# Two attention layers with Fourier mixing: the first transposes, the order of loads and values in the prologue, and the last sums

## The chip, the cores and the metric

The kernel runs on one core of one Trainium2 chip. Its time is device microseconds of one execution; the figure for a kernel is the median of several runs. The core has five engines that each take their own instructions in order: TensorE (PE, its weight loads shown as PEld), VectorE (DVE), ScalarE (ACT), GpSimd (POOL) and SyncE (SP, which here only issues DMA). Engines wait for each other through semaphores. Before the change the median of three runs is 2556.03 us (2554.49 to 2556.99).

## What is computed

Two layers, and each layer is an attention block followed by a Fourier mixing block, both on normalized rows and both added to the residual. There are 2048 rows of 640 columns and 32 heads of 20 columns:

```python
S, D, H = 2048, 640, 32
def A(x, wqkv, wo):
    q, k, v = split(x @ wqkv)                   # 32 heads of 20
    p = softmax(q @ k.T * 20 ** -0.5)
    return concat_heads(p @ v) @ wo
def B(x):                                       # y = Re(DFT_seq(DFT_hidden(x)))
    a, b = x @ hid_re.T, x @ hid_im.T
    return seq_re @ a - seq_im @ b
x = x + A(layernorm(x)); x = x + B(layernorm(x))
x = x + A(layernorm(x)); x = x + B(layernorm(x))
```

Everything is float32. A product that has to be that exact is made of three matmuls on a high part and a low part of each operand (`three`, `passes`); `split` makes the two parts: a rounded copy (ACT, or DVE where it says `vector`), and DVE's difference between the value and that copy.

## The kernel before, in words

All orders are written out by hand: each engine runs its instructions in the order in which the Python code emits them. A layer has these stages: the prologue (`Qkv.prologue`), attention (`Attention.sweep`), the output projection (`Project.run`) and the Fourier block (`Fourier.run`). The code also contains a second, general form of both layers, which runs only if a flag says that the inputs don't have the structure that the fast form uses: at the very end each engine loads the flag (`values_load`, line 1421) and branches over the general form (line 1422).

**The prologue.** The 2048 rows come in eight pairs of 128-row tiles; pair `k` is loaded by `load(k)` into buffer `x{k % 4}` (line 147), so the last two pairs, 6 and 7, go into the buffers of pairs 2 and 3. `stats(k)` takes mean and variance on DVE (L117 to L120) and the inverse root on POOL (L121, L122); `norm(k)` normalizes in place on ACT (L126). The rows are worked on in four blocks of 512 (`tb`), and each block takes two pairs. For a block, `turn(tb)` transposes the four row tiles, one 128 by 128 piece at a time, on PE (L164) into five PSUM banks (`ptr`), one for each 128 columns `dc`, and `split`s each bank into a high part (ACT, L86) and a low part (DVE, L87). Then two products of 15 matmuls each make 128 columns of q and 128 of k (`pqk`, L99). `keep` takes each from PSUM: ACT copies and squares (L193), DVE makes the low part (L194), and POOL issues a store to DRAM (L196). `norms` multiplies the squares with an indicator (`pn`, L201) and DVE takes the maximum (L202). `own` makes the values of one 128-row tile: 15 matmuls (`pv`, L99), one copy on ACT (L234); a block has four of them, 60 matmuls. PSUM has eight banks, taken in turn (`s.bank`), so a new product waits until the readers of the eighth last are done.

The first layer starts from the input in DRAM. Its prologue loads pairs 0 and 1, the weights for q and k, pairs 2 and 3 and the value weights, makes the first two pairs' rows, the q and k weights (`early`), and `turn(0)`. Then it takes statistics of pairs 2 and 3 and normalizes pair 2, ahead of the value weights' split (`values`). In the second layer (`given` is set) the first two pairs come from the Fourier block that has just made them.

The loop over blocks (line 318) is, in the order of emission: loads of the next block but one (`later(tb, k, s.load)`, line 322), q and k with `keep`, with statistics of later pairs between; in the second layer's first block (`late`, line 320) the block's values, with `norm(2)` and `norm(3)` between; then `turn(tb + 1)`; the norms and the `pn` products; SP's loads of q's and k's first tiles from DRAM (`qload`, `kload`, tiles `stq`, `stk`); and, where `late` is not set, the block's values. On SP's queue the loads of pairs 6 and 7 stand in the second block's first place, that is behind the eight transfers of `qload(0, 0, None)` (L486, L487), which wait for q's store.

**The end.** The last step of a Fourier block is `hidden(t)` for eight pairs of row tiles `lo` and `hi`: nine matmuls each (`phid`) make two products `p[0]` and `p[1]` in two banks; `difference_and_sum` copies `p[1]` on ACT (L1180) and makes the difference and the sum on DVE (L1181, L1182); `add` adds them to `lo` on DVE and to `hi` on POOL, 321 columns and then the mirrored 319 (L1190, L1191); SP stores the pair (L1213). The tiles `r0` and `r1` for these parts are taken in turn. Behind the last one come the flag's two instructions on DVE (L1418, L1420), the flag's load on every engine and the branch.

Of the kernel before, what the change touches and what calls it, by code (L numbers as in the profile page):

```python
# [35 lines left out]
def mha_fnet_kernel(ctx, tc, x_in, wqk, wv, wo, seq, hid, nat_seq, nat_hid, out):  # L36
# [41 lines left out]
    def pair(ap, p):  # L78
        return ap.rearrange("(n p) d -> p n d", p=128)[:, p::NP]
# [52 lines left out]
    class Qkv:  # L132
# [24 lines left out]
            s.n += 1  # L157
            return bank(f"b{s.n % 8}", shape, name)

        def turn(s, tb):  # L160
            for dc in range(ND):
                p = s.bank([128, 512], "ptr")
                for i in range(4):
                    PE.transpose(p[:, i * 128:(i + 1) * 128],  # L164
                                 s.xn[2 * tb + i // 2][:, i % 2, dc * 128:(dc + 1) * 128], ident)
                x = s.xtp(f"xt{tb}_{dc}", [2, 512], F32R, "xt")
                s.xt[tb, dc] = [x[:, 0], x[:, 1]]
                split(x[:, 0], x[:, 1], p)
# [95 lines left out]
        def prologue(s, vals, xt, fill, att):  # L264
            s.xtp, s.fill, room = xt, fill, s.room
            if s.given:
                for k in (2, 3):
                    s.load(k)
            s.top = const.tile([128, 2, ND, NB], F32, name="top", bufs=2)
            V.memset(s.top, 0.0)  # L270

            def values():
                s.wv = fill("wv", [ND, 2, HD], F32R, "wv")
                for dc in range(ND):
                    split(s.wv[:, dc, 0], s.wv[:, dc, 1], s.wvraw[dc])

            if s.given:
                s.turn(0)
                values()
            else:  # L280
                s.stats(0)

                s.fetch(0, att.kq, "k3", wait=True)
                s.fetch(ND, att.kq, "k4")
                for k in (2, 3):
                    s.load(k)
                s.load_values()
                s.norm(0)
                s.stats(1)
                s.early(0)  # L290
                s.norm(1)
                s.early(1)
                s.turn(0)
                s.stats(2)
                s.norm(2)
                s.stats(3)
                values()

            def ones(t):
                s.v[t] = vals(f"v{t}", [H * VW + 12], F32, "v")  # L300
                G.memset(s.v[t][:, :H * VW].rearrange("p (a c) -> p a c", c=VW)[:, :, DH:], 1.0)
                G.memset(s.v[t][:, H * VW:], 1.0)

            for t in range(NT - ND):
                ones(t)
            def later(tb, k, f):
                if tb + 2 < NB:
                    f(2 * tb + 4 + k)

            def own(tb, n):  # L310
                t = 4 * tb + n
                p = s.bank([128, HD], "pv")
                for dc in range(ND):
                    for f in s.value(p, t, dc):
                        f()
                s.own(p, t, 0, False)

            for tb in range(NB):

                sq, late = [], s.given and tb == 0  # L320
                for k in range(2):
                    later(tb, k, s.load)
                for k in range(2):
                    p = s.bank([128, 512], "pqk")
                    for dc in range(ND):
                        for f in s.product(p, s.w[k], tb, dc):
                            f()
                    sq.append(s.keep(p, k * ND, tb, False, (room, fill)[k]))
                    if late:
                        s.stats(2 + k)  # L330
                        continue
                    if tb == k == 0:
                        s.norm(3)
                    later(tb, k, s.stats)
                if late:
                    for n in range(4):
                        own(tb, n)
                        if n < 2:
                            s.norm(2 + n)
                            later(tb, n, s.stats)  # L340
                if tb == 0:
                    att.setup()
                elif tb == 1:
                    for t in range(NT - ND, NT):
                        ones(t)
                if tb + 1 < NB:
                    s.turn(tb + 1)
                for k in range(2):
                    later(tb, k, s.norm)
                    s.norms(s.bank([H, 512], "pn"), k * ND, tb, sq[k])  # L350
                if tb == 0:
                    att.qload(0, 0, None)
                elif tb == 1:
                    s.fetch(ND + 1)
                    for j in range(2):
                        att.kload(0, 0, j)
                elif tb == 2:
                    s.w1 = s.weights(s.fill("w", [2, ND, 128], F32R, "wqk"), ND + 1, True)
                    s.fetch(1)
                    att.zeros(room)  # L360
                elif tb == NB - 1:
                    list(s.bound(0, room))
                    att.qshift(0, 0)
                    for j in range(2):
                        att.kload(0, 1, j)
                if not late:
                    for n in range(4):
                        own(tb, n)
            s.made |= {0, ND}
# [660 lines left out]
    class Fourier:  # L1030
# [162 lines left out]
        def hidden(s, t):  # L1193
            lo, hi = s.x[t][:, 0], s.x[t][:, 1]
            o = (t % 4) * 128
            s.nb += 2
            p = [bank(f"b{(s.nb + i) % 8 if t >= NQ else i if t == 3 else 6 + i}", [128, 512], "phid")[:, :HD + 2] for i in range(2)]
            for ri in range(2):
                for c, (_, n) in enumerate(FOLDS[ri]):
                    three(p[ri], [s.u[t // NQ, ri][k][:n, c, o:o + 128] for k in range(2)],  # L1200
                          [s.w[ri, c][:n, k] for k in range(2)], c == 0, c == 2)
            r = s.difference_and_sum(p, s.own(f"r{t % 2}", [3 * (HD + 2)], F32, "r"), 128)
            if t in (0, 2):

# [6 lines left out]
            if t in (0, 2):  # L1211
                G.tensor_copy(hi[0:1], m)
            nc.sync.dma_start(pair(s.dst, t), s.x[t])  # L1213

        def run(s, after):

# [85 lines left out]
    cut = next(i for i, t in enumerate(tasks) if 2 * i >= len(tasks) and isinstance(t, tuple))  # L1302
    tasks = (tasks[:cut], tasks[cut:])

    class Start:


# [8 lines left out]
    def layer(start, src, dst, general, tasks, after):  # L1316
# [1 line left out]
        tag, q, a, vals = start.tag, start.q, start.a, start.vals  # L1318
        p = Project(a, src, d_x[0])
        f = Fourier(p, d_x[0], dst, check)  # L1320
        f.tag = tag
        xt, fill = Pool(f"xt{tag}", "right"), Pool(f"fill{tag}", "right")
        banks(f"q{tag}")
        q.prologue(vals, xt, fill, a)
# [86 lines left out]
    k_ones = d_ones.rearrange("p c -> (p c)").rearrange("(r t) -> r t", r=2)  # L1411
    start.close()

    layers(False, begun)
    banks(None)
    V.tensor_reduce(near[:, 4:5], near[:, 0:3], op=OP.min, axis=AX.X)  # L1418
    flag = const.tile([1, 1], I32, name="flag")
    V.tensor_scalar(flag, near[:, 4:5], 1.0, None, op0=OP.is_equal)  # L1420
    f = nc.values_load(flag[0:1, 0:1], min_val=0, max_val=1)
    with tc.If(f < 1):
        layers(True)
        banks(None)

# [64 lines left out]
```

## Time and profile before

| | |
|---|---|
| median of three runs | 2556.03 us (2554.49 to 2556.99) |
| profiled execution | 2556.55 us |
| its span | 2554.8 us |
| mean granted clock of TensorE | 0.997 |
| busy time PE / PEld | 2512.4 / 1157.5 us |
| busy time ACT / DVE / POOL | 2136.4 / 976.9 / 521.2 us |
| moved by DMA | 262.52 MB, mean 103 GB/s |

The page of the profile describes one execution. A row of the order of time reads: start in us from the span's start, duration, engine, source line, operation, output tile and input tiles, shapes, how many instructions are merged in the row, and in brackets how long the engine sat idle before it and what ended the idleness. A row of the table by stretches reads: the stretch, its length, the busy time of PE, PEld, DVE, ACT and POOL in it (with the number of instructions), the granted clock of TensorE, the busy share of the DMA engines, and GB/s. A row for a source line reads: line, engine (a q behind it: its sequencer), operation, count, shortest, median and longest duration in ns, and start of the first and the last.

### The profile page before, as it was taken

What the parts mean: (1) busy time and instruction counts of PE and PEld (TensorE: products, weight loads), DVE (VectorE), ACT (ScalarE), POOL (GpSimd) and SP (SyncE); (2) the same over time, 40 slices, a digit from 0 to 9 for tenths busy, and PEclk for the clock granted to TensorE, in tenths of its full rate; (3) what the DMA queues carried; (4) which work ended last, traced back from release to release, by engine and by line L of the source; (5) the groups of instructions that cost most, each with busy time, mean ns of one, the idle gap of its engine ahead of it and who ended that gap; (6) DMA issues with size and microseconds to landing.
All of it is one profiled execution on the core that took longest, in us unless ns stands there. A gap on an engine that the chain in (4) does not pass through costs nothing.

```text
span 2554.8 us, 43625 instructions
## 1 busy us (share of the span) xinstructions
PE 2512.4 (98%) x16350; PEld 1157.5 (45%) x16350; DVE 976.9 (38%) x2112; ACT 2136.4 (84%) x2429; POOL 521.2 (20%) x1022
## 2 busy tenths in 40 slices
PE   7999999999999999999999999999999999999998
PEld 6644444433333332239885444444433333322596
DVE  5254422243324233326763444223332322232275
ACT  5588899988999999985456888999899999999752
POOL 2122111121111121114321111111111111131133
PEclk9999999999999999999999999999999999999999
DMA  4233221222323233327452332222221212133365
GB/s 169 99 98 115 86 86 46 82 98 77 101 66 96 73 97 102 116 76 255 181 190 96 104 119 90 69 65 72 82 90 49 77 52 81 51 90 103 103 219 191
DMA packets 127008, 262.52 MB, mean 103 GB/s; under 512 B 28720, under 2 KB 53072, under 8 KB 126788
## 3 DMA queue, kind: packets, MB, share of 16 engines
q1 hardware_dynamic: 88196, 159.79, 19.1%
q0 software_dynamic: 38592, 99.85, 12.4%
q8 instruction: 132, 2.16, 0.4%
q14 instruction: 88, 0.72, 0.1%
HBM read 175.29 MB, written 84.21 MB: 102 GB/s over the span
## 4 chain that ended last, share of the span: by engine, by line
PE 93%; DVE 4%; DMA 1%; ACT 1%; issue 1%; POOL 0%; SPq 0%; DVEq 0%; ACTq 0%
PE acc L519 38%; PE psc L508 28%; PE pqk L99 11%; PE pv L99 6%; PE py L92 2%; PE py L94 2%; PE py L93 2%; PE pn L201 1%; PE pacc L92 1%; PE pacc L93 1%; PE pacc L94 1%; DVE of L526 1%; PE phid L92 1%; PE phid L93 1%; PE phid L94 1%
## 5 line engine op out<-in xcount | busy, mean ns | idle before, releaser
L511 ACT ACTIVATE e<-psc 128x1024 f32<-128x1024 f32 x2048 | 1938.0, 1115 | 156.4 <-PE psc L508 120.2
L519 PE MATMUL acc<-e,v 128*32 128x512 f32 x8192 | 1061.5, 602 | 3.8 <-DVE of L526 3.3
L508 PE MATMUL psc<-stq,stk 62*128 62x512 f32 x4096 | 815.1, 463 | 3.0 <-ACT e L511 3.0
L508 PEld LDWEIGHTS psc<-stq,stk 62*128 62x128 f32 x4096 | 341.3, 184 | 835.4 <-ACT e L511 786.7
L519 PEld LDWEIGHTS acc<-e,v 128*32 128x32 f32 x8192 | 187.5, 108 | 365.8 <-issue 338.3
L540 POOL DMA_DIRECT2D o<-oh x256 | 131.9, 523 | 1000.5 <-DVE oh L535 999.1
L99 PE MATMUL pqk<-xt,wqk 128*128 128x512 f32 x1200 | 313.9, 405 | 3.2 <-DVE wqk L84 1.5
L99 PEld LDWEIGHTS pqk<-xt,wqk 128*128 128x128 f32 x1200 | 215.0, 188 | 88.0 <-issue 37.1
L526 DVE STREAM_TRANSPOSE of<-acc 128x512 f32<-128x512 f32 x64 | 45.9, 716 | 541.8 <-PE acc L519 541.1
L84 DVE CAST hl<-pqk 128x512 fp32r<-128x512 f32 x64 | 44.2, 691 | 454.8 <-PE pqk L99 454.8
L99 PE MATMUL pv<-wv,xt 128*128 128x320 f32 x960 | 161.4, 319 | 2.0 <-DVE hl L194 2.0
L99 PEld LDWEIGHTS pv<-wv,xt 128*128 128x128 f32 x960 | 142.5, 190 | 28.0 <-issue 21.1
L540 POOL DMA_DIRECT2D o<-ot x256 | 128.5, 509 | 1.0 <-issue 0.5
L196 POOL DMA_DIRECT2D scrq<-hl x40 | 28.2, 706 | 388.6 <-DVE hl L87 264.3
L754 DVE TENSOR_REDUCE far<-cq 128x1 f32<-128x512 f32 (+5 forms) x169 | 98.5, 584 | 5.7
L92 PE MATMUL py<-wo,o 128*128 128x320 f32 x320 | 99.2, 310 | 1.4 <-DVE xr L936 1.4
L93 PE MATMUL py<-wo,o 128*128 128x320 f32 x320 | 98.6, 308 | 0.0
L94 PE MATMUL py<-wo,o 128*128 128x320 f32 x320 | 98.6, 308 | 0.0
L758 DVE TENSOR_TENSOR cq<-cq 128x512 f32<-128x512 f32 (+4 forms) x166 | 96.3, 580 | 2.8 <-DMA cq<-in_nat_seq_dram 2.7
L232 DVE COPY v<-pv 128x320 f32<-128x320 f32 x32 | 15.7, 490 | 203.7 <-PE pv L99 203.7
L196 POOL DMA_DIRECT2D scrk<-hl x40 | 27.9, 697 | 297.7 <-DVE hl L87 248.7
L202 DVE TENSOR_REDUCE top<-pn 32x1 f32<-32x512 f32 x80 | 53.4, 675 | 31.3 <-PE pn L201 31.3
(195 smaller groups left out, 1726.3 us busy)
## 6 DMA issues: line engine op xcount, KB each, us to landing
cq<-in_nat_seq_dram POOLq DMA_DIRECT2D x64, 512.0 KB, 5.5
scrq<-hl POOLq DMA_DIRECT2D x40, 512.0 KB, 3.2
scrk<-hl POOLq DMA_DIRECT2D x40, 512.0 KB, 3.5
stq<-scrq SPq DMA_DIRECT2D x256, 80.0 KB
stk<-scrk SPq DMA_DIRECT2D x128, 160.0 KB
o<-o SPq DMA_DIRECT2D x16, 1280.0 KB
stq<-scrq SPq DMA_DIRECT2D x256, 40.0 KB
stk<-scrk SPq DMA_DIRECT2D x128, 80.0 KB
```

The costliest lines, as they stand in the source:

```text
L92: PE.matmul(out_ap, ah, bh, start=start, stop=False)
L93: PE.matmul(out_ap, ah, bl, start=False, stop=False)
L94: PE.matmul(out_ap, al, bh, start=False, stop=stop)
L99: yield lambda i=i, j=j, k=k: PE.matmul(out_ap, a[i], b[j], start=dc == 0 and k == 0, stop=dc == ND - 1 and k == 2)
L196: G.dma_start(s.scr["qk"[k]][c * 128:(c + 1) * 128, :, tb * 512:(tb + 1) * 512], hl.bitcast(F32))
L508: PE.matmul(p[:, i], s.k[g, kc // 8, j][r, kc % 8 * 128:(kc % 8 + 1) * 128], s.q[g, qb, j][r], start=True, stop=True)
L511: A.activation(e, p, AF.Exp, scale=SCALE)
L519: PE.matmul(s.acc[32 * j:32 * j + 32], s.a.v[kc][:, v0:v0 + 32], s.e[n, j // 2][:, j % 2], start=kc == 0, stop=kc == NT - 1, skip_group_ch ...
L526: V.transpose(t0.rearrange("p b c -> p (b c)"), s.acc)
L540: G.dma_start(s.o[k, h * DH:(h + 1) * DH, qb * 512:(qb + 1) * 512], hl[k][32 * j:32 * j + DH])
L754: V.tensor_reduce(to, x, op=OP.max, axis=AX.X, apply_absolute_value=True)
L758: V.tensor_tensor(y, x, y, op=op)
```

## The change

Four edits:

- `turn` gets a form for the first block of the first layer (`wait=True`): all five banks are taken first, the transposes run tile by tile over the five banks instead of bank by bank over the four tiles, and the splits follow as before.
- `late` holds in both layers. In the first layer, too, the statistics of pairs 2 and 3 come behind `keep` of q and of k, and the first block's values come ahead of `turn(1)`, with `norm(2)` and `norm(3)` between them; `stats(2)`, `norm(2)`, `stats(3)` and `norm(3)` are taken out of their former places. The value weights' split then follows `turn(0)` directly.
- In the first block the loads are emitted where they were; for pairs 6 and 7 they are emitted behind `turn(1)`, ahead of `qload`, in both layers.
- The last pair of the last layer gets its own sums (`last`): after the nine matmuls of each product ACT copies it into a part of tile `r1`, POOL adds the copy to the 321 columns of `hi`, and DVE adds or subtracts the product straight from PSUM in three pieces (321 and 319 columns of `lo`, 319 of `hi`). The flag is computed on DVE ahead of them (`decide(0)`) and loaded on all engines ahead of the last store (`decide(1)`), and the store is two DMAs, one for `lo` and one for `hi`.

```diff
-        def turn(s, tb):
+        def turn(s, tb, wait=False):
+            def transpose(p, i, dc):
+                PE.transpose(p[:, i * 128:(i + 1) * 128],
+                             s.xn[2 * tb + i // 2][:, i % 2, dc * 128:(dc + 1) * 128], ident)
+            ps = [s.bank([128, 512], "ptr") for _ in range(ND if wait else 0)]
+            for i in range(4 if wait else 0):
+                for dc in range(ND):
+                    transpose(ps[dc], i, dc)
             for dc in range(ND):
-                p = s.bank([128, 512], "ptr")
-                for i in range(4):
-                    PE.transpose(p[:, i * 128:(i + 1) * 128],
-                                 s.xn[2 * tb + i // 2][:, i % 2, dc * 128:(dc + 1) * 128], ident)
+                if wait:
+                    p = ps[dc]
+                else:
+                    p = s.bank([128, 512], "ptr")
+                    for i in range(4):
+                        transpose(p, i, dc)
...
-                s.turn(0)
-                s.stats(2)
-                s.norm(2)
-                s.stats(3)
+                s.turn(0, wait=True)
                 values()
...
-                sq, late = [], s.given and tb == 0
-                for k in range(2):
-                    later(tb, k, s.load)
+                sq, late = [], tb == 0
+                if late:
+                    for k in range(2):
+                        later(tb, k, s.load)
...
-                    if tb == k == 0:
-                        s.norm(3)
                     later(tb, k, s.stats)
...
                     s.turn(tb + 1)
+                    for k in range(2):
+                        later(tb + 1, k, s.load)
...
+            final = t == NP - 1 and s.dst is out
+            if final:
+                s.end(0)
             for ri in range(2):
                 for c, (_, n) in enumerate(FOLDS[ri]):
                     three(p[ri], [s.u[t // NQ, ri][k][:n, c, o:o + 128] for k in range(2)],
                           [s.w[ri, c][:n, k] for k in range(2)], c == 0, c == 2)
+                if final:
+                    s.last(ri, lo, hi, p[ri])
+            if final:
+                return
...
+        def last(s, ri, lo, hi, p):
+            c = s.own("r1", [3 * (HD + 2)], F32, "r")[:, ri * (HD + 2):(ri + 1) * (HD + 2)]
+            A.activation(c, p, AF.Copy)
+            ops = (OP.subtract, OP.add) if ri else (OP.add, OP.add)
+            G.tensor_tensor(hi[:, :HD + 1], hi[:, :HD + 1], c[:, :HD + 1], op=OP.add)
+            V.tensor_tensor(lo[:, :HD + 1], lo[:, :HD + 1], p[:, :HD + 1], op=ops[0])
+            V.tensor_tensor(lo[:, HD + 1:], lo[:, HD + 1:], p[:, 1:HD], op=ops[1])
+            V.tensor_tensor(hi[:, HD + 1:], hi[:, HD + 1:], p[:, 1:HD], op=ops[0])
+            if ri:
+                s.end(1)
+                for k, x in enumerate((lo, hi)):
+                    nc.sync.dma_start(pair(s.dst, NP - 1)[:, k], x)
...
+    def decide(step):
+        if step == 0:
+            V.tensor_reduce(near[:, 4:5], near[:, 0:3], op=OP.min, axis=AX.X)
+            flag = going["flag"] = const.tile([1, 1], I32, name="flag")
+            V.tensor_scalar(flag, near[:, 4:5], 1.0, None, op0=OP.is_equal)
+            return
+        flag = going["flag"]
+        going["on"] = nc.values_load(flag[0:1, 0:1], min_val=0, max_val=1)
...
-    V.tensor_reduce(near[:, 4:5], near[:, 0:3], op=OP.min, axis=AX.X)
-    flag = const.tile([1, 1], I32, name="flag")
-    V.tensor_scalar(flag, near[:, 4:5], 1.0, None, op0=OP.is_equal)
-    f = nc.values_load(flag[0:1, 0:1], min_val=0, max_val=1)
-    with tc.If(f < 1):
+    with tc.If(going["on"] < 1):
```

More of the change, by code (lines that the diff above doesn't have):

```diff
@@ L1303, in mha_fnet_kernel @@
     tasks = (tasks[:cut], tasks[cut:])
+    going = {}
+    def decide(step):
[6 more added lines that the diff above has]
+        going["on"] = nc.values_load(flag[0:1, 0:1], min_val=0, max_val=1)
     class Start:
@@ L1320, in layer @@
         f = Fourier(p, d_x[0], dst, check)
-        f.tag = tag
+        f.tag, f.end = tag, decide
         xt, fill = Pool(f"xt{tag}", "right"), Pool(f"fill{tag}", "right")
```

## The prediction

> **What bounds the kernel now.** I read the page first, then the order of time around the three places that the diff touches: the first layer's prologue, the second layer's prologue, and the end.
>
> ```profile
> PE 2512.4 (98%) x16350; PEld 1157.5 (45%) x16350; DVE 976.9 (38%) x2112; ACT 2136.4 (84%) x2429; POOL 521.2 (20%) x1022
> ...
> PE 93%; DVE 4%; DMA 1%; ACT 1%; issue 1%; POOL 0%; SPq 0%; DVEq 0%; ACTq 0%
> ```
>
> PE is busy for 98% of the span and holds 93% of the chain that ended last. The change removes no matmul, so all it can win is PE's idle time, PE's slow time, and what follows the last matmul. Whatever is won in a prologue moves everything behind it forward by as much, because there PE simply goes on. First layer, in order of time (start, duration, engine):
>
> ```profile
> 8.22 2.52 SPq L262 DMA_DIRECT2D wvraw<-in_wv_dram  x5
> 10.20 1.72 ACT L126 ACTIVATE xa<-xa,ars 128x640 f32<-128x640 f32 x2
> ...
> 11.97 3.89 PE L164 MATMUL ptr<-ident,xa 128*128 128x128 f32 x17 [0.34 <-ACT xa L126]
> 12.58 0.83 DVE L87 TENSOR_TENSOR wqk<-wraw,wqk 128x640 fp32r<-128x640 f32 x1 [1.43 <-ACT wqk L86]
> 13.32 1.34 DVE L87 TENSOR_TENSOR xt<-ptr,xt 128x512 fp32r<-128x512 f32 x2
> 15.51 7.47 PE L99 MATMUL pqk<-xt,wqk 128*128 128x512 f32 x30
> ...
> 24.92 1.72 ACT L126 ACTIVATE xa<-xa,ars 128x640 f32<-128x640 f32 x2
> 26.70 3.64 PE L164 MATMUL ptr<-ident,xa 128*128 128x128 f32 x17 [0.48 <-ACT xa L126]
> ```
> ```profile
> 39.70 7.00 PE L99 MATMUL pqk<-xt,wqk 128*128 128x512 f32 x30
> ...
> 46.53 2.35 PE L164 MATMUL ptr<-ident,xa 128*128 128x128 f32 x20
> 48.81 0.60 PE L201 MATMUL pn<-sq,ind 128*32 128x512 bf16 x2
> 58.32 7.00 PE L99 MATMUL pqk<-xt,wqk 128*128 128x512 f32 x30
> ```
>
> Seventeen of the first twenty transposes wait for the fourth row tile (ACT's normalization ends at 10.20 + 1.72 = 11.92). The first q/k group ends at 15.51 + 7.47 = 22.98. Then PE has to transpose the second block, whose last two tiles ACT normalizes only at 24.92 to 26.64. The same work by stretches of 2 us (after the stretch: its length, busy time of PE, PEld, DVE, ACT, POOL, then granted clock, DMA share, GB/s):
>
> ```profile
> 22.00:24.00 2.00, 1.20 (x7) 0.75 (x5) 1.35 (x4) 2.00 (x7) 1.92 (x19) 1.00 0.05 12
> 24.00:26.00 2.00, 0.12 (x1) 0.12 (x1) 1.70 (x4) 2.00 (x5) 0.33 (x8) 1.00 0.01 4
> 26.00:28.00 2.00, 1.51 (x7) 1.33 (x8) 1.82 (x8) 2.00 (x4) 0.91 (x1) 0.63 0.25 96
> 28.00:30.00 2.00, 2.00 (x12) 2.00 (x11) 1.97 (x7) 1.49 (x4) 1.61 (x3) 0.51 0.44 166
> ```
>
> PE idles, and then it is given half its clock: a transpose of line 164 takes 3.64/17 = 0.214 us there, against 2.35/20 = 0.118 in the block from 46.53. So a stall costs itself and some 4 us at half rate behind it. The second layer has its values ahead of the second block's rows already:
>
> ```profile
> 1288.24 8.96 PE L99 MATMUL pv<-wv,xt 128*128 128x320 f32 x60
> ...
> 1299.85 7.27 PE L99 MATMUL pqk<-xt,wqk 128*128 128x512 f32 x30
> ...
> 1303.56 0.90 SPq L147 DMA_DIRECT2D xa<-d_x  x2
> ...
> 1304.92 0.69 DVE L194 TENSOR_TENSOR hl<-pqk,hl 128x512 fp32r<-128x512 f32 x1 [1.15 <-ACT sq L193]
> ...
> 1308.73 0.89 DVE L117 BATCH_NORM_STATS2 ast<-xa 128x6 f32<-128x320 f32 x2 [3.12 <-DMA xa<-d_x]
> 1309.23 0.60 PE L201 MATMUL pn<-sq,ind 128*32 128x512 bf16 x2
> ...
> 1311.84 10.71 PE L99 MATMUL pv<-wv,xt 128*128 128x320 f32 x60 [2.01 <-DVE hl L194]
> ...
> 1322.39 6.99 PE L99 MATMUL pqk<-xt,wqk 128*128 128x512 f32 x30
> ```
> ```profile
> 1313.80:1315.80 2.00, 2.00 (x9) 1.77 (x8) 1.89 (x6) 0.76 (x2) 1.43 (x12) 0.50 0.53 201
> ```
>
> Its stall is another. The statistics of the last rows wait 3.12 us for their load; DVE runs in order, so k's low half (L194) queues behind them, k's bank stays taken, and PE idles 2.01 us and then runs at a clock of 0.50. From the pn matmuls to the next q/k group it takes 1322.39 − 1309.23 = 13.16 us; the same stretch in the first layer takes 58.32 − 48.81 = 9.51. The end:
>
> ```profile
> 2543.42 0.31 PE L94 MATMUL phid<-wh,u 65*128 65x322 f32 x1
> ...
> 2543.56 1.10 POOL L1191 TENSOR_TENSOR xd<-xd,r 128x319 f32<-128x319 f32 x1
> 2543.90 0.44 ACT L1180 ACTIVATE r<-phid 128x322 f32<-128x322 f32 x1 [2.24 <-PE phid L94]
> 2544.38 0.49 DVE L1181 TENSOR_TENSOR r<-phid,r 128x322 f32<-128x322 f32 x1 [0.43 <-ACT r L1180]
> ...
> 2545.41 0.88 POOL L1190 TENSOR_TENSOR xd<-xd,r 128x321 f32<-128x321 f32 x1 [0.74 <-issue]
> 2546.24 1.10 POOL L1191 TENSOR_TENSOR xd<-xd,r 128x319 f32<-128x319 f32 x1
> ...
> 2547.37 0.37 SPq L1213 DMA_DIRECT2D out_dram<-xd  x1
> ```
> ```profile
> L1421 SPq TENSOR_LOAD <-flag x1: 502/502/502, 2547.8 to 2547.8; - x1
> ...
> L1422 SPq EVENT_SEMAPHORE  x8: 17/17/17, 2551.8 to 2553.1; - x8
> ...
> L1422 PEldq COMPARE_BRANCH  x1: 4489/4489/4489, 2547.5 to 2547.5; - x1
> ...
> L1422 SPq COMPARE_BRANCH  x1: 50/50/50, 2548.7 to 2548.7; - x1
> ```
>
> POOL's two additions end at 2547.34, SP issues the last store until 2547.74, loads the flag (2547.8), branches at 2548.7, resumes 3.1 us later at 2551.8, and the span ends at 2554.8.
>
> **First transposes tile by tile.** With the tile loop outside, fifteen transposes can go before the fourth tile exists. Tile 3 is ready at 10.20 + 0.86 = 11.06; at the 3.89/17 = 0.229 us of the row, five for it and five for tile 4 end near 13.4, and the first bank is full at 12.4. DVE is free of wqk at 13.41, and makes the low halves 0.67 apart (1.34 for two): 14.1, 14.8 and so on. The second matmul of the q group needs the first of them, and each later group of three takes 0.70 (7.00/30 = 0.233 each), so none waits again. The group ends at 14.1 + 29 × 0.233 = 20.9, a gain of 2.1 us. The other bound: the array is still slow. The clock column shows nothing here, but 0.229 for a transpose is the half rate, and the 7.47 against 7.00 of the q/k rows says that full rate came near 16. Then four or five matmuls run at double cost, and the group ends near 21.7: a gain of 1.3. Between the two rows nothing decides; I take 1.7.
>
> [...]
>
> **Values ahead of the second block in the first layer.** After the change PE's order there is that of the second layer. From the end of the q/k group to the next group it took 39.70 − 22.98 = 16.72 us; in the second layer, from the start of the values, 1299.85 − 1288.24 = 11.61. That wins 5.11, less 0.27 because the next group then follows the transposes at once (7.27 against 7.00): 4.84. What must hold: the value weights are being split when the group ends near 21. Their five loads are issued by 10.74, and this row shows the traffic gone:
>
> ```profile
> 15.00:16.00 1.00, 1.00 (x6) 0.99 (x5) 0.84 (x2) 0.70 (x2) 0.00 (x0) 1.00 0.16 54
> ```
>
> DVE does the splits right behind the five transposed tiles, the last of which starts at 14.1 + 4 × 0.7 = 16.9; five pieces of 320 columns cost no more than five of 512 (0.67 each), so they are done by 21 even at that price, and the first is needed first. The statistics of rows 2 to 5 and ACT's normalizations now lie beside 9 us of value matmuls, as in the second layer, where none stops PE. Low bound 3.5, if one of those loads still stops DVE for a microsecond or so; high bound 5.1.
>
> **Last rows' loads ahead of q's tiles.** SP now waits for the second block's transposes, issues the two loads, and only then q's eight. In the second layer that is near 1299.5 rather than 1303.56. With the old 5.17 us from issue to first use the first load is there at 1304.7, before DVE asks for it (after L194, 1304.92 + 0.69 = 1305.6). The second was issued within 0.9 us of 1303.56 and held neither the next L194 nor the values beyond 1311.84, so it took under about 8 us; it is asked for near 1308.5, 8.6 us after its new issue. So the stretch becomes the first layer's: 13.16 − 9.51 = 3.65 us won. Bounds: 0, if the loads are as late as now, and 3.8. I take 3.65, since the first load's row settles it. Behind the waiting SP stand q's tiles, a weight fetch and k's tiles, none of which PE asks for before attention, some 55 us later. In the first layer the loads were no limit (9.51 with them). There too they now start behind the second block's transposes, some 6.1 us ahead of their first use like here, so what holds here holds there.
>
> **The end in two parts.** The flag is computed ahead of the last additions and loaded on SP ahead of the store. That takes the stretch from 2547.74 to 2548.7 out of the path behind the store: 0.96 us, less 0.05 for the branch itself. The sums win nothing: POOL is on the previous pair until 2543.56 + 1.10 = 2544.66, adds the first copy until 2545.5 (0.88), and ACT's second copy reuses the tile of the first, so it waits for that and ends at 2545.95. DVE's three additions of the second product wait for this copy in the changed program's order of waits, and at 0.49 each (L1181's row) end at 2547.4, where POOL ended before. Two stores of half the size: the second is issued when the one of before was. PE's branch, 4.49 us from 2547.5, now starts behind PE's last matmul, some 2.5 us sooner, and holds nobody. Bounds: −0.9 (each of DVE's three additions slowed to the 1.10 of L1191 by POOL beside it, 1.8 us in all) and 1.4 (DVE doesn't wait for the copy and ends 0.5 sooner). I take 0.9, since every term of it has its row.
>
> [...]
>
> **The sum.** 1.7 + 4.84 + 3.65 + 0.9 = 11.1 us, against the profiled execution of 2556.55 (span 2554.8 and 1.75 around it): 2545.45. The median of the runs, 2556.03, is 0.5 below that execution, so I forecast 2545.0.
>
> **The rivals.** (1) The loads stay late: the SP wait for the transposes or the queue behind it brings the last rows no sooner, and the 3.65 shrinks to about 0.5. For it: these loads took 5 us and more; against it: where they would start the DMA engines are 13% busy.
>
> ```profile
> 1298.00:1300.00 2.00, 2.00 (x16) 1.41 (x14) 1.80 (x7) 2.00 (x5) 0.39 (x1) 1.00 0.13 41
> ```
>
> The time by it: 11.1 − 3.15 = 7.95 saved, 2548. (2) The end turns worse: beside POOL each of DVE's last additions takes 1.10 instead of 0.49 and both stores come later; 0.9 lost instead of 0.9 won: 2547. (3) The change doesn't speed the first layer's turn, because the value weights or rows come late and PE stops at another place: 2545.0 + 4.84 = 2550. Against it is the second layer, which runs this very order without a stop. (4) Slower: the value weights are not split when the first q/k group ends, near 21. Each microsecond later costs one, and after 2 us another 2 at half clock; it would eat all from a readiness of about 30 us on, and at 33 give 2559. The loads land by 16, so little speaks for it.
>
> **How the numbers follow.** Forecast 0.74; rival 1 0.11, rival 2 0.07, rival 3 0.05, rival 4 0.03. The range holds the bounds of the four terms (2.1 + 5.1 + 3.8 + 1.4 = 12.4 below, which is 2543.6, and rival 1 above) and about a microsecond for the scatter of the runs (2554.49 to 2556.99): 2542.5 to 2548.8. About 0.2%, 5.1 us, is what a measurement here tells from no change. The forecast and rivals 1 and 2 are all beyond it, and most of rival 3: faster 0.94, same 0.03, slower 0.03.
>
> **What would show it.** The q/k group of the first layer ends between 20.9 and 21.7; the value matmuls follow without idle, the transposes behind them take 2.35 and not 3.64, with a clock of 1.00 throughout; the next q/k group starts near 33. In the second layer no L117 waits for DMA, and the second block's value matmuls take 9.1 instead of 10.71. SP's branch comes within 0.1 us of the last store. Wrong would be a clock below 1 in either prologue, or a new idle PE ahead of attention.

## The result, and the profile after

The median of six runs of the changed kernel is 2545.31 us (2545.0 to 2545.72), against 2555.88 us (2554.03 to 2556.99) for six runs of the kernel before beside them. The ratio is 0.996, with a 95% interval from 0.9947 to 0.9973. The profiled execution has a span of 2543.2 us, where the one before had 2554.8: 11.6 us less. The first row of the page (busy time by engine):

```profile
PE 2507.9 (99%) x16350; PEld 1153.8 (45%) x16350; DVE 977.0 (38%) x2114; ACT 2136.9 (84%) x2430; POOL 520.3 (20%) x1022
```

The matmuls are as many as before. PE's busy time fell by only 2512.4 − 2507.9 = 4.5 us, most of it in the second block's transposes (3.64 us for seventeen before, 2.35 for all twenty now) and in the second layer's values behind the stall (10.71 before, 9.14 now); the rest of the gain is idle time that is gone. The first layer's prologue in order of time (start, duration, engine):

```profile
8.32 2.39 PE L163 MATMUL ptr<-ident,xa 128*128 128x128 f32 x10 [8.32 <-ACT xa L126]
11.05 1.88 PE L163 MATMUL ptr<-ident,xa 128*128 128x128 f32 x10 [0.33 <-ACT xa L126]
13.18 0.50 PE L99 MATMUL pqk<-xt,wqk 128*128 128x512 f32 x1 [0.25 <-ACT xt L86]
13.95 6.87 PE L99 MATMUL pqk<-xt,wqk 128*128 128x512 f32 x29 [0.27 <-DVE xt L87]
20.66 8.96 PE L99 MATMUL pv<-wv,xt 128*128 128x320 f32 x60
29.45 2.35 PE L163 MATMUL ptr<-ident,xa 128*128 128x128 f32 x20
...
32.26 7.14 PE L99 MATMUL pqk<-xt,wqk 128*128 128x512 f32 x30
```

The first q/k group ends at 13.95 + 6.87 = 20.82, where it ended at 22.98. The values follow without a gap, the second block's transposes take 2.35 us, and the next q/k group starts at 32.26, where it started at 39.70. The granted clock (the third figure from the end of a row by stretches) stays at 1.00 where it had been 0.51:

```profile
28.00:30.00 2.00, 2.00 (x17) 2.00 (x17) 1.61 (x7) 0.50 (x2) 0.49 (x3) 1.00 0.00 0
```

The second layer, PE and the rows of DVE and SP that belong to the last rows:

```profile
1291.85 0.90 SPq L147 DMA_DIRECT2D xa<-d_x  x2
...
1298.06 0.88 DVE L117 BATCH_NORM_STATS2 ast<-xa 128x6 f32<-128x320 f32 x2
1301.77 0.60 PE L212 MATMUL pn<-sq,ind 128*32 128x512 bf16 x2
1302.30 9.14 PE L99 MATMUL pv<-wv,xt 128*128 128x320 f32 x60
1311.28 7.00 PE L99 MATMUL pqk<-xt,wqk 128*128 128x512 f32 x30
```

The loads are issued 6.2 us ahead of their first use (1291.85 to 1298.06), DVE's statistics of these rows wait for nothing, and from `pn` to the next q/k group it takes 1311.28 − 1301.77 = 9.51 us instead of 13.16. The end, first in order of time, then by source line (count, shortest/median/longest in ns, first and last start):

```profile
2531.85 1.04 DVE L1200 TENSOR_TENSOR xd<-xd,r 128x319 f32<-128x319 f32 x1
...
2533.57 0.86 POOL L1236 TENSOR_TENSOR xd<-xd,r 128x321 f32<-128x321 f32 x1
...
2534.47 0.44 ACT L1234 ACTIVATE r<-phid 128x322 f32<-128x322 f32 x1 [2.52 <-POOL xd L1236]
...
2535.74 0.48 DVE L1239 TENSOR_TENSOR xd<-xd,phid 128x319 f32<-128x319 f32 x1
2535.85 1.34 SPq L1243 DMA_DIRECT2D out_dram<-xd  x2
```
```profile
L1459 SPq EVENT_SEMAPHORE  x8: 17/17/17, 2540.9 to 2541.4; - x8
...
L1459 SPq COMPARE_BRANCH  x1: 50/50/50, 2537.2 to 2537.2; - x1
```
```profile
L1521 POOLq DRAIN  x3: 46/107/1784, 2540.6 to 2542.9; - x3
L1521 SPq DRAIN  x3: 7/7/7, 2542.3 to 2542.6; - x3
```

ACT's second copy waits for POOL's first addition, the sums end at 2536.22, the stores are issued until 2537.19, and SP branches at once. But SP goes on only at 2540.9, 3.7 us after its branch, where it had been 3.1. The addition at 2531.85 is DVE's second for the last pair but one; it serves below as the start of the end in every kernel.

### The profile page after: what moved, and what is told of

Same layout as the page of the kernel before. It is cut to its first block, busy times and chain, and to the rows that moved or that the text cites. A ratio compares the mean times of both kernels' runs of the same rounds, so it can differ in the third digit from the quotient of the medians.

```text
span 2543.2 us, 43630 instructions
## 1 busy us (share of the span) xinstructions
PE 2507.9 (99%) x16350; PEld 1153.8 (45%) x16350; DVE 977.0 (38%) x2114; ACT 2136.9 (84%) x2430; POOL 520.3 (20%) x1022
## 3 DMA queue, kind: packets, MB, share of 16 engines
q8 instruction: 132, 2.16, 0.4%
```

## The experiments

Four stretches are read in every profile, so that the parts can be told apart without the scatter of whole runs: (a) from the first transpose's start to the end of the first q/k group; (b) from there to the next q/k group's start; (c) in the second layer from the first block's `pn` to the next q/k group's start; (d) from the start of DVE's 1.04-us addition for the last pair but one to the span's end. In before (d) starts with this row of its order of time:

```profile
2542.91 1.04 DVE L1191 TENSOR_TENSOR xd<-xd,r 128x319 f32<-128x319 f32 x1
```

| kernel | median, us | ratio to before (95%) | (a) | (b) | (c) | (d) |
|---|---|---|---|---|---|---|
| before | 2555.88 | | 14.63 | 16.72 | 13.16 | 11.89 |
| after | 2545.31 | 0.996 (0.9947 to 0.9973) | 12.50 | 11.44 | 9.51 | 11.35 |
| e1_turn_only | 2554.26 | 0.9996 (0.9986 to 1.0005) | 12.90 | 18.80 | 11.71 | 11.31 |
| e2_values_only | 2549.47 | 0.9978 (0.9969 to 0.9988) | 14.22 | 11.44 | 11.11 | 11.28 |
| e3_loads_only | 2552.77 | 0.9991 (0.9981 to 1.0001) | 14.29 | 16.69 | 9.49 | 12.16 |
| e10_fill | 2555.02 | 0.9999 (0.999 to 1.0009) | 14.31 | 15.69 | 12.50 | 11.44 |
| e4_no_load_move | 2547.77 | 0.9972 (0.996 to 0.9984) | 12.62 | 11.44 | 11.64 | 11.41 |
| e5_no_turn | 2547.09 | 0.9969 (0.9957 to 0.9981) | 14.48 | 11.44 | 9.51 | 11.57 |
| e6_old_end | 2546.02 | 0.9963 (0.9949 to 0.9977) | 12.71 | 11.44 | 9.51 | 11.84 |
| e7_flag_early | 2546.2 | 0.9963 (0.995 to 0.9977) | 12.68 | 11.44 | 9.51 | 11.71 |
| e8_one_tile | 2544.72 | 0.9957 (0.9943 to 0.997) | 12.57 | 11.44 | 9.51 | 10.90 |
| e9_one_tile_one_store | 2545.31 | 0.9959 (0.9946 to 0.9973) | 12.65 | 11.44 | 9.51 | 10.82 |
| e11_small_store | 2544.55 | 0.9963 (0.9949 to 0.9977) | 12.89 | 11.44 | 9.52 | 10.47 |
| e12_two_queues | 2545.19 | 0.9963 (0.9949 to 0.9977) | 12.55 | 11.44 | 9.51 | 11.11 |

The median of before was 2555.23 beside e1, e2, e3 and e10 (31 runs), 2555.42 beside e4 to e7, 2556.29 beside e8 and e9, and 2554.81 beside e11 and e12.

### e1_turn_only: the transposes alone

```diff
 # before, with the new form of turn
-                s.turn(0)
+                s.turn(0, wait=True)
                 s.stats(2)
```

> The kernel before with the first transposes tile by tile, nothing else. Theory 1 (the parts depend on each other): the first q/k group ends 2.1 us sooner, at about 20.9, but PE then waits for the second block's rows as before. These hang on DVE's statistics, which stand behind the five low halves; those end only 0.9 us sooner. So the next q/k group starts 0.8 to 0.9 us sooner (near 38.9) and the time falls by 0.8: about 2555. Rival (the parts simply add): 2.1 us less, about 2553.7, and the next q/k group starts near 37.6.

Measured: 2554.26 us, 0.97 below before's 2555.23, near the theory's 0.8, but the interval of the ratio holds 1. The order of time shows what became of it:

```profile
13.39 7.91 PE L99 MATMUL pqk<-xt,wqk 128*128 128x512 f32 x30
21.14 0.74 PE L163 MATMUL ptr<-ident,xa 128*128 128x128 f32 x2
25.12 0.47 PE L163 MATMUL ptr<-ident,xa 128*128 128x128 f32 x1 [3.24 <-ACT xa L126]
25.93 3.89 PE L163 MATMUL ptr<-ident,xa 128*128 128x128 f32 x17 [0.34 <-ACT xa L126]
29.75 1.04 PE L212 MATMUL pn<-sq,ind 128*32 128x512 bf16 x2
30.72 9.54 PE L99 MATMUL pv<-wv,xt 128*128 128x320 f32 x60
40.10 7.00 PE L99 MATMUL pqk<-xt,wqk 128*128 128x512 f32 x30
```

The group ends at 21.30 instead of 22.98, 1.68 sooner, but the second block's last rows come only 0.77 sooner (25.93 instead of 26.70), about what the theory had, and PE idles 3.24 us instead of 2.68. The 0.77 is then lost in longer rows: the seventeen transposes take 3.89 us instead of 3.64 (0.229 each, where the block from 46.53 in before has 0.118), the `pn` products 1.04 instead of 0.60, the values 9.54 instead of 9.06. In before the clock stood at 0.63 from 26 to 28 and at 0.51 from 28 to 30; what it was in e1 isn't shown. So the next q/k group starts at 40.10, which is 0.40 later than before, and this edit alone wins nothing in the prologue of this execution. That the span is 1.5 us shorter nevertheless comes from stretches that the edit doesn't touch, (c) above all.

### e5_no_turn: the change without the new transposes

```diff
-                s.turn(0, wait=True)
+                s.turn(0)
```

> The changed kernel with the first transposes bank by bank again. Theory 1: the first q/k group ends at about 22.98 instead of 20.82, nothing behind it waits for anything but PE, and all of it shows: 2.1 us more, about 2547.4. Rival (what the order wins is hidden behind the splits): under 1 us more, below 2546.3.

Measured: 2547.09, 1.78 above the changed kernel, which is the theory's 2547.4 rather than the rival's figure. Stretch (b) is 11.44 us with and without the edit. Once values stand behind the q/k group, what it ends sooner is kept.

### e2_values_only: the values alone

```diff
-                s.stats(2)
-                s.norm(2)
-                s.stats(3)
                 values()
...
-                sq, late = [], s.given and tb == 0
+                sq, late = [], tb == 0
...
-                    if tb == k == 0:
-                        s.norm(3)
```

> The kernel before with the values ahead of the second block's rows in the first layer, nothing else; the last rows' loads stay behind q's tiles. Theory 1: in the first layer q's store has landed early, so q's eight transfers are through before the second block's transposes end, the loads are not late, and the whole 5.1 to 5.3 us come: about 2550.6, with no statistics waiting for DMA in the first layer. Rival: as in the second layer before, the loads stand behind q's transfers and DVE waits for them, about 3.7 us are lost again in the first layer, and the time is near 2554.3, with a clock of 0.5 in that stretch.

Measured: 2549.47, 5.76 below before's 2555.23: the theory's 2550.6 with a microsecond more, and far from the rival's. Stretch (b) falls from 16.72 to 11.44 with the loads where they were, so in the first layer the place of the loads sets nothing.

### e10_fill: how much of it is the clock

In before, 22 more transposes of the identity (work that the kernel doesn't need) ahead of the second block's, in the first layer, so that PE doesn't idle while it waits:

```diff
                 p = s.bank([128, 512], "ptr")
+                for i in range(22 if tb == 1 and dc == 0 and not s.given else 0):
+                    PE.transpose(p[:, :128], ident, ident)
```

> The kernel before with 22 transposes of the identity on PE ahead of the second block's transposes in the first layer, into the bank that these fill next; their results are overwritten. PE stays busy where it waited for ACT. Theory 1 (the wait costs twice, once as idle time and once as half the clock behind it): the granted clock stays 1.00 between 22 and 30 us, the transposes from 26.7 on take 0.12 us each instead of 0.214, and the next q/k group starts 1.5 us sooner: about 2554.4. Rival (the slow transposes are held by ACT's and DVE's splits of the banks): no change, 2555.9.

Measured: 2555.02 against 2555.23, no difference that the runs can tell (the interval reaches some 2.5 us either way). The profile tells one. PE and the clock there:

```profile
25.84 0.33 PE L166 MATMUL ptr<-ident,xa 128*128 128x128 f32 x1 [0.53 <-ACT xa L126]
26.65 2.08 PE L166 MATMUL ptr<-ident,xa 128*128 128x128 f32 x17 [0.48 <-ACT xa L126]
...
38.38 3.82 PE L99 MATMUL pqk<-xt,wqk 128*128 128x512 f32 x16
```
```profile
26.00:28.00 2.00, 1.52 (x13) 1.35 (x13) 1.82 (x9) 2.00 (x5) 0.91 (x1) 1.00 0.29 109
```

The clock stays at 1.00, where it had been 0.63, and the seventeen transposes take 2.08 instead of 3.64, though the rows come when they did (26.65 against 26.70). The next q/k group starts 39.70 − 38.38 = 1.32 us sooner, where the theory had 1.5; (b) falls by 16.72 − 15.69 = 1.03, because here the first group happened to end 0.29 sooner. So of the 5.28 us that the values win, 1.0 to 1.3 is half clock and the rest is waiting that is now filled with needed work.

### e3_loads_only and e4_no_load_move: the loads

e3 is before with the loads of pairs 6 and 7 moved in both layers; e4 is the changed kernel with this taken back.

```diff
 # e3, to before; e4 takes the same move back (there the condition reads `if late:`)
-                for k in range(2):
-                    later(tb, k, s.load)
+                if tb == 0:
+                    for k in range(2):
+                        later(tb, k, s.load)
...
                     s.turn(tb + 1)
+                    for k in range(2):
+                        later(tb + 1, k, s.load)
```

> The kernel before with the last rows' loads ahead of q's tiles in both layers, nothing else. Theory 1: only the second layer wins: its pn products to the next q/k group take 9.5 us instead of 13.2, 3.7 us less in all, about 2552.2; the first layer's prologue keeps its length within 0.3 us. Rival: q's tiles, now behind the loads, are late for attention and give some back: above 2553.5.

> The changed kernel with the last rows' loads back behind q's tiles, in both layers. Theory 1 (only the second layer needs the move): 3.7 us more than the changed kernel, about 2549.0; in the second layer the statistics wait some 3 us for DMA, the values start 2 us late and run at half clock at first; in the first layer nothing changes. Rival (with values ahead, both layers need it): 7.3 us more, about 2552.6.

Measured: e3 2552.77, 2.46 below before; e4 2547.77, 2.46 above the changed kernel. Both lie nearer to the theory, and both are short of its size, more than a microsecond in e4. With the move (c) is 9.49 to 9.52 in every kernel; without it, it is 13.16, 11.71, 11.11, 12.50 and 11.64. Those five follow how late the load is and how long PE idles for it ahead of the values: 2.01, 1.44, 0.83, 2.23 and 1.37 us. Less this idle (c) is 11.15 us in before and 10.27 to 10.28 in the other four. Before has a clock of 0.50 behind its idle and stands 0.66 above e10, which idled longer and has 1.00. In e4:

```profile
1296.55 0.90 SPq L147 DMA_DIRECT2D xa<-d_x  x2
```
```profile
1301.10 0.89 DVE L117 BATCH_NORM_STATS2 ast<-xa 128x6 f32<-128x320 f32 x2 [2.48 <-DMA xa<-d_x]
```
```profile
1304.21 2.46 PE L99 MATMUL pv<-wv,xt 128*128 128x320 f32 x15 [1.37 <-DVE hl L205]
1307.18 6.86 PE L99 MATMUL pv<-wv,xt 128*128 128x320 f32 x45 [0.51 <-DVE xt L87]
```

From the end of the issues to the statistics it takes 1301.10 − 1297.45 = 3.65 us here, PE idles 1.37 us, and the values behind it take 2.46/15 = 0.164 and 6.86/45 = 0.152 us each (9.14/60 = 0.152 in after). In the profile of before it was 4.27 us, 2.01 us of idle, a clock of 0.50 behind it, and 10.71/60 = 0.179 us for a matmul of the values. The move is worth the mean of the five less 9.51, that is 12.02 − 9.51 = 2.5 us, which is also what both medians show; the 3.65 of the prediction was one execution's. (The interval of e3 alone still holds 1.)

### e6_old_end and e7_flag_early: the end

e6 is the changed kernel with before's end. e7 has before's sums and its single store, and the flag computed and loaded ahead of that store.

```diff
 # e7, to the changed kernel
-                if final:
-                    s.last(ri, lo, hi, p[ri])
-            if final:
-                return
...
+            if final:
+                s.end(1)
             nc.sync.dma_start(pair(s.dst, t), s.x[t])
```

> The changed kernel with the old end (sums by difference and sum, one store, flag behind it). By the two traces the new end is worth 0.5 us of the span, so 2545.8. Rival (the recorded estimate): 0.9 us more, 2546.2.

> The changed kernel with the old sums and one store, but with the flag computed ahead of the sums and loaded ahead of the store. Theory 1: what the end won is the flag alone, and the second store costs 0.5 us of issue behind the first; without it SP branches 0.4 us sooner: 2544.9. Rival (the sums in two parts win something themselves): at or above the changed kernel's 2545.3.

Measured: e6 2546.02, between the two figures, so it decides nothing alone. e7 2546.2: the theory fell, the early flag wins nothing against e6. The rows of SP in e7:

```profile
L1443 SPq EVENT_SEMAPHORE  x8: 17/17/17, 2541.9 to 2542.4; - x8
...
L1443 SPq COMPARE_BRANCH  x1: 50/50/50, 2537.3 to 2537.3; - x1
```

The branch is early, as foreseen, but SP goes on 4.6 us behind it, where it was 3.1 in before. This table gives for each kernel the time in us from the start of (d), read off its rows (those by source line are given to 0.1 us); POOL's drain is its longest, 1.784 us:

| kernel | sums end | last store issued | SP branches | SP goes on | POOL's drain ends | span ends |
|---|---|---|---|---|---|---|
| before | 4.43 | 4.83 | 5.79 | 8.89 | 10.37 | 11.89 |
| e6_old_end | 4.43 | 4.83 | 5.74 | 8.94 | 11.02 | 11.84 |
| e7_flag_early | 4.43 | 4.84 | 4.91 | 9.51 | 9.69 | 11.71 |
| after | 4.37 | 5.34 | 5.35 | 9.05 | 10.53 | 11.35 |
| e5_no_turn | 4.37 | 4.83 | 4.87 | 9.37 | 10.65 | 11.57 |
| e8_one_tile | 3.69 | 4.61 | 4.70 | 8.50 | 10.08 | 10.90 |
| e9_one_tile_one_store | 3.69 | 4.15 | 4.22 | 8.22 | 9.90 | 10.82 |
| e11_small_store | 4.43 | 4.83 | 4.87 | 7.67 | 9.65 | 10.47 |
| e12_two_queues | 3.69 | 4.15 | 3.71 | 7.51 | 10.19 | 11.11 |

With the sums of before or of after and the whole last store to move (the first five rows), SP goes on 8.9 to 9.5 us after the start, whether it branched at 4.9 or at 5.8. Two chains can end last. In before and e7 the span ends 1.5 and 2.0 us behind POOL's drain, and SP is last; in the other seven it ends 0.8 to 0.9 behind that drain. Before and e6 have the same end, and the distance is 1.52 us in the one and 0.82 in the other, so the chain that is last differs between these two executions. POOL's drain in its turn ends 5.8 to 6.5 us behind POOL's own branch in all nine (branch at 2547.5 in before, 2536.1 in e7 and in after, for example).

### e11_small_store: what SP waits for behind its branch

e7 with the last store cut to 8 of 128 partitions; the other rows of the last pair are not written.

```diff
-            nc.sync.dma_start(pair(s.dst, t), s.x[t])
+            few = 8 if final else 128
+            nc.sync.dma_start(pair(s.dst, t)[:few], s.x[t][:few])
```

> The kernel with the flag computed and loaded early, the old sums and one last store (2546.2 us, profiled span 2544.1), with that store cut to 8 of 128 partitions; the other rows of the last pair of tiles are not written. In its uncut profile SyncE branched at 2537.3, 0.9 us sooner than with the old end (2538.1), but went on only at 2541.9, 4.7 us after the store's issue ended (2537.23), while the store's traffic shows until 2540. Theory: what follows SyncE's branch waits until the last store has been moved, so an earlier flag wins nothing; with next to nothing to move SyncE goes on some 3.1 us after its branch, as before the change (2548.7 to 2551.8), that is by 2540.4, and the end is then GpSimd's, whose 1.78-us drain ended at 2542.1: span about 2543.0, time about 2545.1. Rival: the 4.6 us after the branch are the branch's own, whatever the store moves: span 2544.0, time 2546.1.

Measured: 2544.55 us, span 2542.4. SP's rows, then POOL's drains:

```profile
L1444 SPq EVENT_SEMAPHORE  x8: 17/17/17, 2539.6 to 2540.1; - x8
...
L1444 SPq COMPARE_BRANCH  x1: 50/50/50, 2536.8 to 2536.8; - x1
```
```profile
L1506 POOLq DRAIN  x3: 46/107/1784, 2539.8 to 2542.2; - x3
```

SP goes on 2.8 us behind its branch instead of 4.6, and (d) is 10.47 instead of 11.71. So the rival falls: the 4.6 us are not the branch's own, for 1.8 of them went with the store. That SP waits for the store's last bytes, as the theory has it, is not shown. In before SP went on at 2551.8. The last store is the last issue of its queue there, and of that queue five packets still started between 2552 and 2553 (packets, MB, share of the DMA engines):

```profile
q1 hardware_dynamic: 5, 0.01, 2.6%
```

How the store delays SP stays open. With the small store the end is POOL's, as the theory had it: its drain ends at 2539.8 + 1.78 = 2541.6, 0.8 before the span does, the distance that e6, after and e8 show too.

What the 2.8 us are that are left with next to nothing to store isn't shown, and that a whole store ahead of SP's branch makes it 4.6 us stands on this pair of runs alone.

### e8_one_tile, e9_one_tile_one_store and e12_two_queues: the sums

e8 gives both of ACT's copies parts of one tile taken once, so that the second doesn't wait for POOL. e9 is e8 with one store for both halves. e12 is e8 with the second half's store issued by ACT.

```diff
 # e8
-            c = s.own("r1", [3 * (HD + 2)], F32, "r")[:, ri * (HD + 2):(ri + 1) * (HD + 2)]
+            if not ri:
+                s.both = s.own("r1", [3 * (HD + 2)], F32, "r")
+            c = s.both[:, ri * (HD + 2):(ri + 1) * (HD + 2)]
 # e9, to e8
-                for k, x in enumerate((lo, hi)):
-                    nc.sync.dma_start(pair(s.dst, NP - 1)[:, k], x)
+                nc.sync.dma_start(pair(s.dst, NP - 1), s.x[NP - 1])
 # e12, to e8
-                for k, x in enumerate((lo, hi)):
-                    nc.sync.dma_start(pair(s.dst, NP - 1)[:, k], x)
+                nc.sync.dma_start(pair(s.dst, NP - 1)[:, 0], lo)
+                nc.scalar.dma_start(pair(s.dst, NP - 1)[:, 1], hi)
```

> The changed kernel with one tile for both copies in the last sums, taken once, so that ACT's second copy need not wait for POOL's first addition. Theory 1 (the copy waits for the tile): ACT's second copy starts right behind PE's last matmul, 1.9 us sooner, DVE's six additions run back to back, end 0.6 us sooner, and the time is 0.5 to 0.6 us less: 2544.7. Rival (POOL's last branch, not the sums, ends the span): the sums end sooner and the time stays within 0.2 of 2545.3.

> As the kernel with one tile for both copies, and with one store of the last pair instead of two. Theory 1 (SP's issue and branch end the span): SP branches 0.5 us sooner still, 2544.2. Rival (another engine's branch ends the span by then): no better than with two stores.

> The changed kernel with one tile for both of ScalarE's copies (2544.7 us, profiled span 2542.9), the second half of the last store issued by ScalarE instead of SyncE. There SyncE's two issues took 1.29 us together and its branch came at 2536.7. Theory: the end follows two chains that lie within 0.1 us of each other, SyncE's (branch, semaphores, its drain at 2541.9) and GpSimd's (branch at 2535.8, drain until 2542.1); SyncE's branch comes some 0.9 us sooner, but GpSimd's chain stays where it was: time within 0.2 us of 2544.7. Rival: SyncE's chain alone sets the end, and the time falls by 0.5 us or more, to 2544.2 or less.

Measured: e8 2544.72, as the theory had it, and the lowest time of a kernel that does all the work. Its second copy no longer names POOL:

```profile
2532.86 0.44 ACT L1236 ACTIVATE r<-phid 128x322 f32<-128x322 f32 x1 [0.76 <-PE phid L94]
...
2535.21 0.48 DVE L1241 TENSOR_TENSOR xd<-xd,phid 128x319 f32<-128x319 f32 x1
```

The sums end 0.68 us sooner than in after (3.69 against 4.37), POOL branches 0.4 sooner (2535.8 here is 3.8 after the start, 2536.1 in after is 4.2), and POOL's drain and the end come 0.45 sooner. e9 takes 2545.31, so its theory fell: SP branches 0.48 sooner than in e8, and (d) is the same within 0.1. e12 takes 2545.19: SP branches another half microsecond sooner and goes on 1.0 sooner than in e8, and nothing is won, so its rival fell; that it lies 0.5 above e8 is more than its theory's 0.2. In e8, e9 and e12 it is POOL's chain (branch, semaphores, drain) that ends last, and what e9 and e12 change on SP does not move it. By the medians the gain of the single tile itself is uncertain: e9 and e12 have the same sums as e8 and take 2545.31 and 2545.19, against 2545.31 for the changed kernel.

## Why the prediction was right, point by point

**The whole.** Forecast 2545.0 us, measured 2545.31, within the range; the sum of 11.1 us stands against 11.6 between the two profiles and 10.6 between the medians. Part of the agreement is luck. With the sizes found below the sum is 1.7 + 5.14 + 2.5 + 0.2 = 9.5 us, and the forecast was taken from a before of 2556.03, where the median of 31 runs is 2555.23: a start that was too high and a saving that was too large cancel in part. Of the signs that the prediction names, the clock and the lengths came. Two small ones did not: a row of L117 in the second layer (1289.61, for earlier rows) still waits 0.23 us for DMA, which PE doesn't notice, and PE idles 0.25 and 0.27 us around the first q/k matmul, which (a) contains.

**First transposes: +1.7, right in mean.** The two profiles give 2.16, just beyond the high bound of 2.1, but the profile of before had the longest of its kind. Over nine profiles with the edit and five without, (a) is 12.67 and 14.39 in the mean: 1.7. The two bounds are both seen: full rate from the start (after, 29 matmuls in 6.87 us) and a slow start (e1, 30 in 7.91). The prediction didn't say that this term hangs on the next: in e1, alone, the prologue gains nothing, and in e5 the edit is worth 1.8 behind the values.

What decides between a fast and a slow start isn't shown: (a) spreads from 12.50 to 12.90 over the nine profiles with the edit, and from 14.22 to 14.63 over the five without.

**Values ahead: +4.84, right.** (b) fell by 16.72 − 11.44 = 5.28 us, where 5.11 was taken from the second layer's order. What was to be paid back was 7.14 − 7.00 = 0.14 instead of 0.27, so 5.14 are left where 4.84 was forecast. The value weights were in time, as argued: no idle ahead of 20.66. Rivals 3 and 4 are out.

**Loads ahead: +3.65, right as a mechanism and for the profiled pair, too large for a typical execution.** The stretch became the first layer's 9.51, and the wait on the load is gone, so rival 1 is out. In the first layer the loads were no limit, as said (e2, e3). What was mis-sized is the stall of before: 13.16 us in the profile used, 11.11 to 12.50 in four others with the same order of loads. The step that failed was to take a DMA wait from one execution, and the loss of the clock behind it, as if they were a fixed price; the mean gives 2.5.

**The end: +0.9, wrong in its reason.** The prediction's step "That takes the stretch from 2547.74 to 2548.7 out of the path behind the store: 0.96 us" failed. SP's branch did come right behind the last store (2537.19 and 2537.2), but that stretch was not on the path: e7 shows the branch 0.83 sooner than in e6 and the end 0.13 sooner. In e6 POOL's drain ended last, and in e7 SP waited longer behind its earlier branch; e11 shows that the size of the store has a part in this wait (2.8 us with the small store, 4.6 with the whole one). The premise that the second store is issued when the old one was also failed in the profile of after: its two issues took 1.34 us, until 5.34 instead of 4.83; in e5, the same code there, they took 0.83, and the end was no sooner. The sums were foreseen rightly (ended 0.06 sooner), with ACT's wait for POOL (2.52 us) and DVE's for ACT's copy (0.59 us). In place of the 0.9 stand 0.54 between the two profiles, and 0.2 between the mean of six profiles with before's end (11.65) and of three with the change's (11.44). The six lie between 11.28 and 12.16, so whether the end won anything is within their scatter, and what the halved store does stays open. Rival 2 did not happen: DVE's additions took 0.48 beside POOL.

## What to carry to other kernels

Work that PE finished sooner counted here only where what followed didn't wait for something else: the new transposes are worth 1.78 us behind the values (e5) and nothing in the prologue without them (e1). Fill the wait first (here with the block's values), and only then speed up what lies ahead of it. A stall on a DMA read off one profile is a sample: (c) took 11.11 to 13.16 us in five profiles with the same order of loads. Look at the same stretch in several executions before it goes into a sum at full size. At the end of this program the branch over unrun code and the last store were not in series as their order in the queue suggests: in e7 SP branched 0.83 us sooner than in e6, and the end came 0.13 sooner. Find the engine whose chain ends last before shortening another's.

## What the runs showed of the hardware

- About the same idle time cost the clock in one profile and not in another. In the second layer before lost it after 2.01 us of idle (0.50 in the prediction's row from 1313.80 on); e10, with 2.23 us at the same place, kept it, as the row below of the table by stretches shows. What decides isn't settled here.

```profile
1312.00:1313.00 1.00, 1.00 (x9) 1.00 (x8) 0.86 (x4) 1.00 (x2) 0.00 (x0) 1.00 0.50 188
1313.00:1314.00 1.00, 0.50 (x4) 0.24 (x3) 1.00 (x4) 0.02 (x1) 0.71 (x1) 1.00 0.88 336
```

- Behind the branch over the unrun form SP went on after 2.8 us in e11, with 8 of 128 partitions of the last pair to store, and after 3.1 to 4.6 us in the first five rows of the table of the end, with all of the pair's 640 KB; in those five it waited the longer the sooner it branched, to within 0.1 us. POOL's drain took 1.784 us in every profile, and where it ended last the span ended 0.8 to 0.9 us behind it.
- Loading the flag took 465 to 543 ns on every engine in before, and 1056 to 1058 ns on ACT, DVE and POOL in after, where each of them is loading it among its last additions and copies:

```profile
L1346 PEldq TENSOR_LOAD <-flag x1: 486/486/486, 2533.2 to 2533.2; - x1
...
L1346 POOLq TENSOR_LOAD <-flag x1: 1058/1058/1058, 2534.9 to 2534.9; - x1
```
